# A one-element Gelu behind the last Exp, and one transposition placed a projection later

## The chip, the cores and the metric

The kernel runs on one core of a Trainium2 chip. The metric is the device time of one launch in microseconds (us). Three launches of the kernel before took 168.78, 169.01 and 170.12 us, so their median is 169.01 us. Trace times below count from the start of the profiled span.

## The reference

Attention over four batches with eight heads, 768 positions and a head size of 64, followed by a gated MLP block on its output. Attention keeps, for each query, the last 128 positions and the first four (sinks).

```python
scores = scale * np.matmul(q, k.transpose(0, 1, 3, 2))
scores = np.where(is_sink | in_window, scores, -1e9)
a = softmax(scores)
x = (a @ v)                     # as (4, 768, 512)
h = gelu_tanh(x @ w_in)         # w_in: 512 x 1024
u, v = h[..., :512], h[..., 512:]
v_n = (v - mean(v)) / sqrt(var(v) + 1e-6) * g_ln
v_s = einsum('ts,bsd->btd', w_sg, v_n) + b_sg
out = x + (u * v_s) @ w_out
```

## The kernel before

The 32 heads are worked off as 16 pairs (`n` = 0 to 15), four pairs to a batch, so "the fifteenth pair" is `n` = 14 and the last is 15. For each pair the kernel turns k and q so that the head size lies on the partitions, multiplies them into scores for three groups of keys (`score`), takes the exponential on ScalarE (L277, group 2 last), masks the band on VectorE and GpSimd (`keep_band`), and multiplies by v (`values(n, c)`, c = 0 and 1 for the two halves of the queries). `values` ends on VectorE: a reciprocal (L328) and a product that writes `x` (L329). Before the MLP can use `x` it has to be transposed into `xT`: by a DMA for pairs 8, 9, 12 and 13, and otherwise by `turn_x`, which is six transposing matmuls on TensorE into one bank (`xps`, L337) and one copy on VectorE or ScalarE (L341 or L339).

When a batch's four pairs are there, `hidden(b)` runs. `hidden_v` makes six tiles of the second half of h: four matmuls each over the chunks c = 0 to 3 of `xT` (three of them at L361, the last at L368), a Gelu on ScalarE into `v_all` (L370), and two statistics on VectorE (L372 `st`, L373 `mv`). Of these tiles the first three are opened ahead of time by `open_v`, which does L361 without L368. Then `hidden_u` makes eight half-width tiles of the first half (L380) with a Gelu each (L383, `uT`). `inverse_root` and `normalise` (L393 to L408, `vn`) are VectorE's. `spatial` multiplies `vn` by the turned `w_sg` (L418, six matmuls a tile, the sixth of which needs the sixth `vn`) and gates on VectorE (L421 `gv`, L424 `gT`). `project` multiplies by `w_out` (L449, four matmuls) and adds `x`, either on VectorE (L452) or by a fifth matmul (L455) with a copy on ScalarE (L458), and sends the tile out.

For batches 0 to 2, `spatial` and `project` are not run at once: they are put in a list, `fillers`, and `fill(k)` runs the next k of them between the steps of the next batch's attention. In the last batch the list holds, when the loop over pairs ends, projections of the batch before; those that add on VectorE come first and the three that copy on ScalarE last. The last call `fill(3)` inside `hidden(B - 1)` runs these three.

The schedule is manual: every engine runs its instructions in the order in which this code issues them. All TensorE results except scores go through four PSUM banks (`bank`, pool `ps_m`), given out in turn: a new tile waits until the tile four before it has been read. `hidden_v`, `turn_x`, `values`, `spatial` and `project` all take theirs from there.

ScalarE's functions need a table. In the loop it holds the one for Exp; the Gelus need another, loaded by an instruction of ScalarE (`ACT_TABLE_LOAD`) that the compiler places, so it carries the line of the instruction that it stands ahead of: L370, L277 or L223.

Around the change the order before, issued in the iteration n = 15 and behind the loop, is: a projection (called A here), `turn_x(14)`, then `fill()` (projection B), `values(15, 0)`, `values(15, 1)`, a third projection (C), `open_v` for tiles 0 and 1, `turn_x(15)`, `open_v` for tile 2, and `hidden`. A, B and C all add on VectorE.

Of the kernel before, what the change touches and what calls it, by code (L numbers as in the profile page):

```python
# [8 lines left out]
F32 = mybir.dt.float32  # L9
BF16 = mybir.dt.bfloat16  # L10
I32 = mybir.dt.int32
AF = mybir.ActivationFunctionType
# [6 lines left out]
def kernel(  # L19
# [15 lines left out]
    V, G, A = nc.vector, nc.gpsimd, nc.scalar  # L35
# [11 lines left out]
    NP = B * HP  # L47
# [9 lines left out]
    small = ctx.enter_context(tc.tile_pool(name="small", bufs=4))  # L57
# [15 lines left out]
    ones = consts.tile([128, 1], BF16, name="ones")  # L73
# [36 lines left out]
    def load_all(n):  # L110

        for which, m in (("k", n), ("q", n), ("v", n - 1)):
            if m < NP:
                load(m, which, in_rows=m >= FIRST)

    def cast_all(n, parts="kqv"):
        for which in parts:
            m = n - 1 if which == "v" else n
            if m < NP:
                cast(m, which, G)  # L120
# [27 lines left out]
    for i in range(WARM):  # L148
# [3 lines left out]
        out=halves[:, :, 0, :], in_=halves[:, :, 0, :], compare_op=ALU.is_ge, fill=DARK,  # L152
        base=0, pattern=[[0, 2], [1, 128]], channel_multiplier=-1)
    G.affine_select(
        out=halves[:, :, 1, :], in_=halves[:, :, 1, :], compare_op=ALU.is_ge, fill=DARK,
# [42 lines left out]
    def turn_weights(si, eng):  # L198
        ps = bank([128, NT, 128], BF16, "wps")
        for ti in range(NT):  # L200
            nc.tensor.transpose(ps[:, ti, :], wsg_sb[ti // HT][:, ti % HT, 128 * si:128 * (si + 1)],
                                iden)
        if eng is A:
            A.copy(wsgT[:, si, :], ps.rearrange("p t c -> p (t c)"))
        else:
            eng.tensor_copy(wsgT[:, si, :], ps.rearrange("p t c -> p (t c)"))


    def bank(shape, dtype, name):
        return ps_m.tile(shape, dtype, name=name, tag="m")  # L210
# [4 lines left out]
    def columns(n, which, eng):  # L215
        src = flat.pop((n, which))
        ps = bank([128, NT, 128], BF16, which + "ps")
        for t in range(NT):
            nc.tensor.transpose(ps[:, t, :], src[:, t, :], iden)  # L219
        dst = work.tile([128, S], BF16, name=which + "T")  # L220
        o, i = dst.rearrange("c (p t) -> c p t", t=NT), ps.rearrange("c t p -> c p t")
        if eng is A:
            A.copy(o, i)  # L223
        else:
            eng.tensor_copy(o, i)  # L225
        (kTs if which == "k" else qTs)[n] = dst
# [72 lines left out]
    def begin_x(b):  # L299
        x_sb[b] = work.tile([128, HP, NT, 128], BF16, name="x", bufs=3)  # L300
        xT[b] = work.tile([128, HP, S], BF16, name="xT")

    def values(n, c):
        b, hp = divmod(n, HP)
        if hp == 0 and c == 0:
            begin_x(b)
        ex, v_sb = exps[n], v_bufs[n % NV]
        av = bank([128, HT, 2, 65], F32, "av")

        def probs(j, l, half):  # L310
            at = 512 * l + 256 * (j % 2) + 128 * half
            return ex[:, j // 2, at:at + 128]

        first = True
        for m in range(HT):
            i = HT * c + m
            for l in range(2):
                for j, half in ((i, 0), (i - 1, 1)):
                    if j >= 0:
                        nc.tensor.matmul(av[:, m, l, :], probs(j, l, half), v_sb[:, l, j, :],  # L320
                                         start=first, stop=False)
                        first = False
        for l in range(2):
            sinks = ex[:, HT - 1, 512 * l + 384:512 * (l + 1)]
            to, of = (av[:, 2, l, :], 0) if c == 0 else (av[:, :, l, :], slice(1, 4))
            nc.tensor.matmul(to, sinks, vsink[:, of, n, l, :], start=False, stop=l == 1)  # L326
        rcp = rcps[:, n, c].rearrange("p (i l o) -> p i l o", l=2, o=1)
        V.reciprocal(rcp, av[:, :, :, 64:65])  # L328
        V.tensor_mul(  # L329
            x_sb[b][:, hp, HT * c:HT * (c + 1), :].rearrange("p i (l d) -> p i l d", l=2),  # L330
            av[:, :, :, 0:64], rcp.to_broadcast([128, HT, 2, 64]))

    def turn_x(n, eng):
        b, hp = divmod(n, HP)
        ps = bank([128, NT, 128], BF16, "xps")
        for t in range(NT):
            nc.tensor.transpose(ps[:, t, :], x_sb[b][:, hp, t, :], iden)  # L337
        if eng is A:
            A.copy(xT[b][:, hp, :], ps.rearrange("p t c -> p (t c)"))  # L339
        else:  # L340
            eng.tensor_copy(xT[b][:, hp, :], ps.rearrange("p t c -> p (t c)"))  # L341
# [33 lines left out]
    def hidden_u(b, f, n):  # L375
# [3 lines left out]
        for c in range(KD):  # L379
# [3 lines left out]
        A.activation(out=uTs[b][:, f, NH * n:NH * (n + 1)],  # L383
                     in_=h_ps[:, 0:NH], func=AF.Gelu_apprx_tanh)

    def inverse_root(b):

        w = small.tile([128, NT], F32, name="w", bufs=2)
        h = small.tile([128, NT], F32, name="h", bufs=2)
        s = small.tile([128, NT], F32, name="s", bufs=2)  # L390
        si = small.tile([128, NT], I32, name="si", bufs=2)
        y = small.tile([128, NT], F32, name="y", bufs=2)
        V.tensor_scalar(out=w, in0=mvs[b][:, :, 1], scalar1=1e-6, scalar2=None, op0=ALU.add)  # L393
        V.tensor_single_scalar(out=si, in_=w.bitcast(I32), scalar=1,
                               op=ALU.logical_shift_right)
        V.tensor_scalar(out=h, in0=w, scalar1=-0.5, scalar2=None, op0=ALU.mult)
        V.tensor_scalar(out=y.bitcast(I32), in0=si, scalar1=-1.0, scalar2=float(0x5f3759df),
                        op0=ALU.mult, op1=ALU.add)
        for _ in range(3):
            V.tensor_mul(s, y, y)  # L400
            V.tensor_mul(s, s, h)
            V.scalar_tensor_tensor(out=y, in0=s, scalar=1.5, in1=y, op0=ALU.add, op1=ALU.mult)
        rstds[b] = y
# [154 lines left out]
    def fill(count=1):  # L558
        for _ in range(count):
            if fillers:  # L560
                fillers.pop(0)()
# [117 lines left out]
    def x_by_dma(n):  # L679
        return n >= 2 * HP and n % HP < HP - 2  # L680
# [3 lines left out]
    for n in range(HP, NP):  # L684
        todo = valued < n - 1
        block = n % HP == 0 and n > HP
        if HP < n <= 2 * HP:
            load_all(n + 3)
        if n not in exps:
            score(n, 0, 1)  # L690
        if n == HP:
            for si in range(3, NT):
                turn_weights(si, V)
        keep_band(n, 0, V)
        keep_band(n, 1, G)
        if n + 2 >= FIRST:
            cast_all(n + 2, "kq")
        if todo:
            values(n - 1, 0)
        fill(2 if n > HP and not todo else 1)  # L700
        if n + 1 < FIRST and not block:
            columns(n + 1, "k", A)
        if n == HP:
            columns(n + 1, "q", V)
            fill()
        score(n, 2)
        keep_band(n, 2, G)
        if todo:
            values(n - 1, 1)
            if x_by_dma(n - 1):  # L710
                turn_x_by_dma(n - 1)
        if FIRST <= n + 2 < NP:
            columns_by_dma(n + 2)
            if n + 4 == FIRST + 2:
                load_all(n + 4)
        if QUOTA[n] > 2 and todo:
            fill()
        if HP < n < FIRST - 1 and not block:
            columns(n + 1, "q", A if todo else V)
        if n + 2 <= NP:  # L720
            cast_all(n + 2, "v" if n + 2 >= FIRST else "kqv")
        if QUOTA[n] > 1:
            fill()
        if block:
            open_v(n // HP - 1, 0)
            open_v(n // HP - 1, 1)
        if todo and not x_by_dma(n - 1):
            turn_x(n - 1, V)
        if block:
            open_v(n // HP - 1, 2)  # L730
        valued = n - 1
        if block:
            hidden(n // HP - 1, {1: [lambda: values(n, 0)], 3: [lambda: values(n, 1)],
                                 5: [lambda: columns(n + 1, "k", A)] if n + 1 < FIRST else [],
                                 6: [lambda m=m: load_all(m) for m in later.get(n, ())],
                                 7: [lambda: columns(n + 1, "q", A)] if n + 1 < FIRST else [],
                                 9: [lambda: turn_x_by_dma(n) if x_by_dma(n) else turn_x(n, V)],
                                 LAST: [lambda: score(n + 1, 0, 1), lambda: fill(2)]})
            valued = n
    fill()  # L740
    values(NP - 1, 0)
    values(NP - 1, 1)
    fill(len(fillers) - 3)
# [49 lines left out]
```

## Time and profile before

| what | us |
|---|---|
| median of three runs | 169.01 |
| profiled execution, whole | 168.79 |
| its span, first to last instruction | 167.0 |
| TensorE matmul busy | 155.6 (93%) |
| VectorE busy | 131.8 (79%) |
| ScalarE busy | 109.1 (65%) |
| GpSimd busy | 78.1 (47%) |
| table loads on ScalarE | 8, each 1.283 |
| span from 127.19 (last Exp ends) to 134.84 | ScalarE idle, 7.66 |

The span is 1.8 us shorter than the execution's time. The granted TensorE clock has a mean of 0.993 of full speed and is 1.00 in every stretch from 127 to 162 us. A matmul's end in the trace is modelled, and matmuls overlap: a start 0.216 us after the start before it is full pace for 512 columns and 0.162 us for 384, while the printed durations are 0.38 and 0.33. An idle time in brackets stands ahead of the instruction, with the one that ended it.

### The profile page before, as it was taken

The page shows a single profiled execution, that of the slowest core. Times are in us where ns is not written, and L with a number is a line of the kernel's source. Part 1 is how long each engine was busy: PE and PEld are TensorE (multiplying, and loading weights), DVE is VectorE, ACT ScalarE, POOL GpSimd, SP SyncE. Part 2 cuts the span into 40 slices and gives each one's busy share as a digit, 9 for nine tenths or more (in the row PEclk, how much of TensorE's full clock was granted, in tenths as well). Part 3 has the DMA queues.
Part 4 walks back from the last instruction along what each step waited for, and adds up shares of the span by engine and source line. Part 5 has one row for each costly group of instructions (what it writes and reads, how often), then busy time and mean ns, then how long its engine had stood idle before and what let it go on. Part 6 is the DMA issues. An engine that isn't in the chain of part 4 may idle for free.

```text
span 167.0 us, 4051 instructions
## 1 busy us (share of the span) xinstructions
PE 155.6 (93%) x1558; PEld 91.1 (55%) x1558; DVE 131.8 (79%) x317; ACT 109.1 (65%) x148; POOL 78.1 (47%) x115
## 2 busy tenths in 40 slices
PE   3979999999999999999999999999999989999960
PEld 3535574666567665565665655554565635545530
DVE  6756874996899986799888994989999939887620
ACT  3198878889977689688887367679754068621130
POOL 6479771105899979400289996001985000000000
PEclk9999999999999999999999999999999999999997
DMA  4999979999999979999903999899931310050343
GB/s 140 329 323 263 205 104 282 213 317 287 283 220 296 279 247 351 295 215 224 205 20 67 132 238 210 190 228 216 177 76 34 130 63 0 0 194 2 122 151 122
DMA packets 60194, 31.09 MB, mean 186 GB/s; under 512 B 48356, under 2 KB 57080, under 8 KB 60168
## 3 DMA queue, kind: packets, MB, share of 16 engines
q1 hardware_dynamic: 56800, 27.47, 68.8%
q0 software_dynamic: 2944, 2.77, 10.3%
q10 hardware_dynamic: 424, 0.53, 0.9%
q8 instruction: 14, 0.23, 0.6%
q14 instruction: 12, 0.10, 0.2%
HBM read 24.81 MB, written 6.29 MB: 186 GB/s over the span
## 4 chain that ended last, share of the span: by engine, by line
PE 70%; DVE 17%; DMA 5%; issue 1%; ACT 1%; SPq 1%; POOL 1%; POOLq 0%; ACTq 0%
PE vs L418 13%; PE o_ps L449 10%; PE hu L380 9%; PE hv L361 8%; PE av L320 7%; PE sc L264 6%; DMA k_sb<-in_k_dram 5%; DVE gT L424 3%; DVE gv L421 3%; PE hv L368 3%; PE xps L337 2%; DVE st L372 2%; PE av L326 2%; PE qps L219 2%; PE kps L219 2%; DVE vn L408 2%
## 5 line engine op out<-in xcount | busy, mean ns | idle before, releaser
L277 ACT ACTIVATE ex<-sc 128x1024 bf16<-128x1024 f32 x48 | 47.5, 1024 | 12.7 <-PE sc L264 9.2
L418 PE MATMUL vs<-wsgT,vn 128*128 128x384 bf16 x192 | 35.5, 326 | 0.1
L294 POOL TENSOR_SCALAR_AFFINE_SELECT ex<-ex 128x512 bf16<-128x512 bf16 x25 | 17.0, 680 | 30.7 <-issue 15.2
L418 PEld LDWEIGHTS <-vn 128*128 128x128 bf16 x192 | 17.7, 98 | 10.7 <-DVE tot L480 0.4
L449 PE MATMUL o_ps<-w_out_sb,gT 128*128 128x512 bf16 x92 | 23.5, 379 | 0.0
L380 PE MATMUL hu<-xT,w_in_sb 128*128 128x384 bf16 x128 | 22.1, 326 | 0.0
L421 DVE SCALAR_TENSOR_TENSOR gv<-vs,g_sb,b_bc 128x384 bf16<-128x384 f32 x32 | 19.6, 612 | 3.1 <-PE vs L418 2.7
L372 DVE BATCH_NORM_STATS2 st<-v_all 128x6 f32<-128x512 f32 x24 | 16.1, 671 | 5.8 <-ACT v_all L370 5.8
L361 PE MATMUL hv<-w_in_sb,xT 128*128 128x512 bf16 x72 | 18.8, 379 | 0.7 <-ACT v_all L370 0.7
L107 POOL CAST k_bf<-k_sb 128x768 bf16<-128x768 f32 x15 | 13.1, 870 | 13.0 <-DMA k_sb<-in_k_dram 9.0
L329 DVE TENSOR_TENSOR x<-av,rcps 128x384 bf16<-128x384 f32 x32 | 17.8, 557 | 1.1
L424 DVE TENSOR_TENSOR gT<-gv,uT 128x384 bf16<-128x384 bf16 x32 | 17.0, 532 | 1.9
L383 ACT ACTIVATE uT<-hu 128x384 bf16<-128x384 f32 x32 | 15.7, 493 | 4.1 <-PE hu L380 3.7
L458 ACT COPY o_sb<-o_ps 128x512 f32<-128x512 f32 x13 | 7.4, 593 | 14.3 <-PE o_ps L455 12.8
L264 PE MATMUL sc<-qT,kT 64*128 64x256 bf16 x192 | 15.7, 264 | 1.1 <-DVE qT L225 0.7
L380 PEld LDWEIGHTS <-w_in_sb 128*128 128x128 bf16 x128 | 12.3, 98 | 8.0
L370 ACT ACTIVATE v_all<-hv 128x512 f32<-128x512 f32 x24 | 13.1, 600 | 5.0 <-PE hv L368 4.6
L320 PE MATMUL av<-v_sb,ex 128*128 128x65 bf16 x352 | 16.1, 194 | 0.0
L104 POOL CAST v_sb<-v_sb 128x768 bf16<-128x768 f32 x16 | 14.5, 909 | 2.4 <-DMA v_sb<-in_v_dram 2.4
L320 PEld LDWEIGHTS <-ex 128*128 128x128 bf16 x352 | 13.1, 98 | 4.3 <-issue 1.1
L107 POOL CAST q_bf<-q_sb 128x768 bf16<-128x768 f32 x15 | 13.9, 925 | 2.9 <-DMA q_sb<-in_q_dram 2.9
L296 POOL TENSOR_SCALAR_AFFINE_SELECT ex<-ex 128x512 bf16<-128x512 bf16 (+1 forms) x25 | 14.4, 574 | 0.0
(88 smaller groups left out, 218.0 us busy)
## 6 DMA issues: line engine op xcount, KB each, us to landing
k_sb<-in_k_dram SPq DMA_DIRECT2D x16, 384.0 KB, 6.0
v_sb<-in_v_dram SPq DMA_DIRECT2D x16, 384.0 KB, 6.3
out_dram<-o_sb SPq DMA_DIRECT2D x23, 256.0 KB, 2.3
q_sb<-in_q_dram SPq DMA_DIRECT2D x15, 384.0 KB, 5.7
wsg_sb<-in_moe_w_sg_dram POOLq DMA_DIRECT2D x2, 576.0 KB, 10.9
w_in_sb<-in_moe_w_in_dram POOLq DMA_DIRECT2D x2, 256.0 KB, 6.4
w_in_sb<-in_moe_w_in_dram POOLq DMA_DIRECT2D x1, 512.0 KB, 5.4
w_out_sb<-in_moe_w_out_dram POOLq DMA_DIRECT2D x1, 512.0 KB, 9.3
```

The lines of the kernel that those rows point to most:

```text
L107: eng.tensor_copy(dst.rearrange("p t (h d) -> p h t d", h=2), src)
L264: nc.tensor.matmul(sc[:, 512 * l + w:512 * l + w + n_q], kT[rows, 128 * j:128 * (j + 1)], qT[rows, 128 * j:128 * j + n_q], start=not dark, ...
L277: A.activation(out=exps[n][:, g, :], in_=sc, func=AF.Exp, scale=scale)
L320: nc.tensor.matmul(av[:, m, l, :], probs(j, l, half), v_sb[:, l, j, :], start=first, stop=False)
L329: V.tensor_mul(x_sb[b][:, hp, HT * c:HT * (c + 1), :].rearrange("p i (l d) -> p i l d", l=2), av[:, :, :, 0:64], rcp.to_broadcast([128, HT ...
L361: nc.tensor.matmul(hvs[b, j], xT[b][:, c, 128 * j:128 * (j + 1)], w_in_sb[:, c, DF:], start=(c == 0), stop=False)
L372: V.bn_stats(out=st, in_=v_alls[b][:, j, :])
L380: nc.tensor.matmul(h_ps[:, 0:NH], w_in_sb[:, c, 128 * f:128 * (f + 1)], xT[b][:, c, NH * n:NH * (n + 1)], start=(c == 0), stop=(c == KD - 1))
L418: nc.tensor.matmul(vs[:, 0:NH], vns[b][:, si, 128 * f:128 * (f + 1)], wsgT[:, si, cols], start=(si == 0), stop=(si == NT - 1))
L421: V.scalar_tensor_tensor(out=gv, in0=vs[:, 0:NH], scalar=g_sb[:, f:f + 1], in1=b_bc[:, cols], op0=ALU.mult, op1=ALU.add)
L424: V.tensor_mul(gTs[b][:, f, cols], gv, uTs[b][:, f, cols])
L449: nc.tensor.matmul(o_ps, gTs[b][:, c, rows], w_out_sb[:, c, :], start=(c == 0), stop=(c == KU - 1 and not by_act))
```

## The change

```diff
+    def draw_gelu():
+
+        few = small.tile([1, 1], F32, name="few", bufs=1)
+        A.activation(out=few, in_=ones[0:1, :], func=AF.Gelu_apprx_tanh)
...
-        if todo and not x_by_dma(n - 1):
+        if todo and not x_by_dma(n - 1) and n < NP - 1:
             turn_x(n - 1, V)
...
             valued = n
+    draw_gelu()
     fill()
+    turn_x(NP - 2, V)
     values(NP - 1, 0)
     values(NP - 1, 1)
     fill(len(fillers) - 3)
```

Behind the loop over pairs, ScalarE gets one Gelu of a single element, whose result nothing reads. `turn_x(14)`, last in the iteration n = 15, is issued one projection later: the order becomes A, B, `turn_x(14)`, `values(15, 0)`, `values(15, 1)`, C. The Gelu's input `ones` was written at the start of the kernel.

In the instruction order of the two builds, ScalarE's stream gets one instruction more and the same number of table loads: the load that stood ahead of the first `v_all` of the last batch stands ahead of the one-element Gelu. Before, the load itself waited for TensorE and VectorE; it now waits for nothing, and the first `v_all` carries the waits. TensorE's six transpositions stand behind projection B's four matmuls, and VectorE's copy `xT` stands behind projection B's add. Nothing else changes place on any engine or queue. The branch that is taken only for inputs out of bounds keeps its work.

## The prediction

> **What bounds the kernel now.** I read the chain of waits first, for the stretch behind the last Exp. Its columns are start, length and what ran.
>
> ```profile
> 134.40 0.39 PE hv L368
> 134.79 0.03 ACTq L370
> 134.81 0.03 issue
> 134.84 1.28 ACT L370
> 136.12 0.01 issue
> 136.14 0.61 ACT v_all L370
> 136.74 0.02 issue
> 136.77 0.70 DVE st L372
> ...
> 145.24 2.83 DVE vn L408 x6
> 148.07 0.07 DVE tot L480
> 148.14 4.23 PE vs L418 x25
> ```
>
> The table load of 1.28 us lies on the chain: it starts when the first hv is written and the Gelu starts 0.02 behind it. From 136.77 to 148.07 VectorE runs without a gap to the sixth vn; there TensorE takes the chain over and, by the later rows, holds it to 161.47, when one copy and a DMA are left. Next is the timeline, to see how far TensorE trails VectorE at that handover, and how an earlier batch did it.
>
> ```profile
> 103.18 2.31 ACT L370 ACTIVATE v_all<-hv 128x512 f32<-128x512 f32 x4 [0.79 <-PE hv L368]
> 134.84 1.28 ACT L370 ACT_TABLE_LOAD   x1 [7.66 <-PE hv L368]
> 135.69 0.38 PE L368 MATMUL hv<-w_in_sb,xT 128*128 128x512 bf16 x1
> 136.78 0.81 PE L361 MATMUL hv<-w_in_sb,xT 128*128 128x512 bf16 x3 [0.72 <-ACT v_all L370]
> 146.73 0.38 PE L455 MATMUL o_ps<-x,iden 128*128 128x512 bf16 x1
> 147.14 5.23 PE L418 MATMUL vs<-wsgT,vn 128*128 128x384 bf16 x30
> ```
>
> In the third batch the load ran at 101.11, before hv was due, and the first Gelu began 0.42 behind the start of hv's last matmul (102.76 to 103.18). In the last batch that distance is 1.76 (134.38 to 136.14). TensorE suffers too: its fifth hv tile waits for the bank that the first Gelu reads.
>
> Last, the timeline around the moved transposition.
>
> ```profile
> 128.41 0.56 DVE L329 TENSOR_TENSOR x<-av,rcps 128x384 bf16<-128x384 f32 x1
> 129.02 0.34 PE L337 MATMUL xps<-iden,x 128*128 128x128 bf16 x3 [0.28 <-DVE x L329]
> 129.80 0.68 DVE L452 TENSOR_TENSOR o_sb<-o_ps,x 128x512 f32<-128x512 f32 x1
> 130.40 0.55 DVE L341 COPY xT<-xps 128x768 bf16<-128x768 bf16 x1
> 130.54 0.53 PE L320 MATMUL av<-v_sb,ex 128*128 128x65 bf16 x12
> 130.87 0.68 DVE L452 TENSOR_TENSOR o_sb<-o_ps,x 128x512 f32<-128x512 f32 x1
> 131.07 1.02 PE L449 MATMUL o_ps<-w_out_sb,gT 128*128 128x512 bf16 x4
> ```
>
> TensorE waits 0.28 for x, but VectorE has no gap here: it goes from one row into the next. That decides the second part.
>
> **The change part by part.** *The Gelu.* Load and Gelu go where ScalarE sits idle for 7.66 us (127.19 to 134.84). The load is 1.28. A one-element Gelu is not in the trace: nothing from below, since it is an added instruction, and 0.37 from above (the smallest ScalarE row, the copy of 256 columns at L441); I take 0.2, from the 493 ns of 384 columns and 1024 ns of 1024, which extrapolate to 0.17 at none. Together 1.5 of 7.66, so 6.2 us of cover remain and the cost is nothing. Were that cover gone, it would be 1.5 on ScalarE's path. No ScalarE work is queued behind them before the first v_all, which now waits itself; the row for such a wait is the 0.03 + 0.03 between hv and the load, paid already. Its bounds are 0.06 saved and 0.06 added; I take zero. So the first v_all comes at 136.14 - 1.30 = 134.84 if hv is no later.
>
> The Trainium skill, ScalarE: Activation LUTs, section What ACT_TABLE_LOAD costs, puts a switch at 1283 ns for the load and about 1380 ns more for a drain, some 2.66 us. The load's 1.283 agrees; the 0.02 between its end and the Gelu, and the 0.03 of issue ahead of it, leave no room for the drain here. By the page the sum would gain an estimated 1.38 us more.
>
> *The transposition.* A's four matmuls start at 127.55, so B's start at 127.55 + 4 x 0.216 = 128.41. B takes a bank that a gv read free at 127.61 (127.00 + 0.61). B ends its share at 129.28, x was written at 128.97, so the 0.28 wait is gone and the six transpositions end by about 129.65. But the second values(15) tile takes A's bank, which A's add frees at 129.80 + 0.68 = 130.48. It started at 130.54 before and cannot start sooner now: the 0.28 turns into a wait for that add. Then projection C, which took the bank of xps (free at 130.95), takes B's, freed by B's add. On VectorE the add and the copy trade places: add 130.40 to 131.08, copy about 131.00 to 131.55; the reciprocal behind them stays at 131.47. So C starts at about 131.08 + 0.05 = 131.13 where it started at 131.07: 0.06 lost. The first open_v takes the bank of xps, free at 131.55, and starts at 131.94 + 0.06 = 132.00, with 0.45 to spare; its third matmul, the first to read the moved xT, has more. x of the last pair is written at 132.94 as before, ahead of its transposition at 133.29. The move is therefore worth -0.06, with bounds of +0.20 (if TensorE were free of VectorE, x at 132.94 would let the last transposition start near 133.0, not 133.23) and -0.45.
>
> *What it sums to.* hv is 0.06 later, so the first v_all is at 134.90, 1.24 earlier. VectorE has v_all tiles in time (six in 3.17, while its own statistics take 0.81 a tile and a 1.1 us count lies between), so the sixth vn ends at 148.07 - 1.24 = 146.83. TensorE: the fourth hv's last matmul starts at 135.69, so without the bank wait the fifth tile starts at 135.69 + 0.216 = 135.90, plus 0.06 = 135.96; the bank is free at about 134.90 + 0.61 + 0.02. The gain is 136.78 - 135.96 = 0.82, for the hu tiles and the three projections alike, as no row between shows TensorE waiting for the statistics. TensorE's first vs matmul moves from 147.14 to 146.32 and the sixth would be 5 x 0.162 behind it, at 147.13. vn is there at 146.83. So TensorE, not VectorE, now sets the end, and its sixth vs matmul moves from 148.14 to 147.13: 1.01 us. Everything behind is TensorE's chain, with VectorE following it at 0.98 a tile, so the shift goes through to the last DMA. What is late next is TensorE itself, by 0.3 us.
>
> 168.79 - 1.01 = 167.78 us, against the profiled execution. That execution is 0.22 below the median of the runs, so a median is likelier between 167.8 and 168.0.
>
> **The rivals.** *Nothing lands, 168.85.* The compiler puts the load where a table is needed; a second load ahead of v_all, or a wait left on the load, would leave 134.84 to 136.12 as it is and add the 0.06 of the move. For it: in the batch before the change the load carried the wait itself. Against: the eight loads of the profile stand one to a change of function; six v_all, eight uT and the copies between run on one, as at 101.11, and in the built order the only load left stands ahead of the small Gelu. The Trainium skill, ScalarE activation tables: per-element evaluation and per-set limits, section Table sets in the compiler and the runtime, has the loads placed per block by the longest run, which fits these rows.
>
> *More, 167.55 or less.* VectorE's 1.24 comes through whole if TensorE makes up 0.23 between 136 and 147. For it: the count's matmul (L478) starts 0.31 behind L455 rather than 0.216, and some such pauses may close. Against: TensorE's rows from 138.51 to 147 follow each other at full pace. The drain of the page, as a mechanism here, would be 1.38 between load and Gelu; the 0.02 speaks against it, and I give it 1 in 100 within this case.
>
> *Slower, 169.4.* One mechanism: projection B, now ahead of the transpositions, finds its bank not yet free. If it got A's turn of banks and waited for A's add (130.48), B would start at 130.53. From B's start to the first open_v it is 0.86 + 0.34 + 1.01 + 0.86 = 3.07 at the pace of the rows (projection, transpositions, values from 130.06 to 131.07, projection): 133.60 in place of 131.94. That is 1.66 lost; ScalarE's part alone still gives 0.88 + 0.19 = 1.07 (TensorE's bank wait, and the 148.14 - 147.95 that it now waits for vn), so 0.59 slower. It costs something once B starts later than about 131.94 + 0.06 - 3.07 = 128.93, and makes the kernel slower once later than 131.94 + 1.07 - 3.07 = 129.94. Against: banks go round by four and B's was freed at 127.61. For: these rounds are tight, as A's bank shows.
>
> **How the numbers follow.** The forecast gets 0.65; nothing lands 0.12; more 0.13; slower 0.10. The forecast's own range is 167.5 to 168.1 by the bounds above, of which the move's ends are the widest, with 0.2 for the median. The range of 167.3 to 169.0 adds the no-gain case and most of "more", and leaves out the slower one. One per cent of the median, about what a measurement of this kernel can tell from no change, is 1.69 us: below 167.32 lies part of "more" and a low draw of the forecast, 0.10; above 170.70 lies the tail of "slower", 0.06; the rest, 0.84, is within.
>
> **What would show it.** In the profile after: the load behind the last Exp at about 127.2; no load ahead of the last batch's v_all, and that v_all near 134.9; no wait of the fifth hv tile for ScalarE; the sixth vn near 146.8 and TensorE not waiting for it; C at 131.1 and open_v at 132.0. Wrong would be a first vs matmul still at 147.1, which says that TensorE kept its place, or VectorE still ahead of the sixth vs in the chain, which is "more".

## The result and the profile after

The changed kernel takes 167.95 us (median of 14 runs, 167.29 to 169.05) against 168.88 us for the kernel before, measured beside it. The ratio is 0.994, with a 95% interval of 0.992 to 0.996: 0.9 us faster, with 167.8 forecast for the profiled execution. Some executions of the versions below were slower as a whole, by 1.5% or more, and the ratios leave them out. The profiled execution takes 167.96 us, 0.83 less than the one before; its span is 166.15 us in the trace, where it was 166.95 (the table of the profile before rounds it to 167.0). Lines behind the new function are five to seven higher: L418 is now L423, L449 is L454.

The chain of waits, for the stretch shown before (start, length, what ran):

```profile
133.63 0.65 PE hv L361 x3
134.28 0.01 issue
134.28 0.82 PE hv L368 x3
...
137.69 5.20 PE hu L380 x32
...
146.22 4.98 PE vs L423 x30
```

ScalarE and VectorE are gone from this stretch. TensorE runs from hv through hu, the three projections and all thirty vs matmuls without a break. The timeline shows where the load went:

```profile
127.03 1.28 ACT L389 ACT_TABLE_LOAD   x1
...
128.33 0.20 ACT L389 ACTIVATE few<-ones 1x1 f32<-1x1 bf16 x1
...
134.76 2.71 ACT L370 ACTIVATE v_all<-hv 128x512 f32<-128x512 f32 x5 [6.23 <-issue]
...
135.80 0.81 PE L361 MATMUL hv<-w_in_sb,xT 128*128 128x512 bf16 x3
...
143.87 2.83 DVE L413 TENSOR_SCALAR vn<-v_all,mv,y 128x512 bf16<-128x512 f32 x6
...
146.16 5.05 PE L423 MATMUL vs<-wsgT,vn 128*128 128x384 bf16 x30
```

The fifth hv tile (135.80) has no wait for ScalarE any more. The six vn end at 143.87 + 2.83 = 146.70, and TensorE takes the sixth 0.81 behind 146.16. And the moved transposition:

```profile
127.37 1.89 PE L454 MATMUL o_ps<-w_out_sb,gT 128*128 128x512 bf16 x8
...
129.10 0.50 PE L337 MATMUL xps<-iden,x 128*128 128x128 bf16 x6
...
129.64 1.28 DVE L457 TENSOR_TENSOR o_sb<-o_ps,x 128x512 f32<-128x512 f32 x2
...
130.38 0.53 PE L320 MATMUL av<-v_sb,ex 128*128 128x65 bf16 x12 [0.41 <-DVE o_sb L457]
...
130.84 0.55 DVE L341 COPY xT<-xps 128x768 bf16<-128x768 bf16 x1
...
130.97 1.02 PE L454 MATMUL o_ps<-w_out_sb,gT 128*128 128x512 bf16 x4
```

A and B run as one row of eight, the wait for x is gone, and in its place TensorE waits 0.41 for A's add. This add is the one VectorE step left on the chain behind the last Exp.

Executions differ in what happens before this stretch. Projection A's first matmul stands between 127.36 and 127.82 in eleven of the thirteen profiled executions of this study, and at 128.75 and 128.79 in the other two (e4 and e5 below). In those two the granted TensorE clock was 0.50 from 14 to 16 us, where the other eleven have 1.00; their executions took 169.80 and 169.49 us, about 1 us more than the medians of the same versions. What moves the other eleven by up to 0.5 us was not followed up. So the traces are compared from A's first matmul on:

| from A's first matmul | before | forecast change | measured change |
|---|---|---|---|
| to projection C | 3.52 | +0.06 | 3.60, +0.08 |
| to the first v_all | 8.59 | -1.24 | 7.39, -1.20 |
| to the fifth hv tile | 9.23 | -0.82 | 8.43, -0.80 |
| to the first vs matmul | 19.59 | -0.82 | 18.79, -0.80 |
| to the last copy on ScalarE ("the stretch") | 33.94 | -1.01 | 32.96, -0.98 |
| from that copy to the end of the span | 5.46 | 0 | 5.82, +0.36 |

With A itself 0.18 earlier, 0.18 + 0.98 - 0.36 = 0.80 us is the difference of the two spans. Of these three only the 0.98 is in the forecast's sum. The 0.18 is chance: the changed kernel, run again (after_again below), has A at 127.59.

### The profile page after: what moved, and what is told of

It reads as the page before. It is cut to its first block, busy times and chain, and to the rows that moved or that the text cites. A ratio compares the mean times of both kernels' runs of the same rounds, so it can differ in the third digit from the quotient of the medians.

```text
span 166.1 us, 4052 instructions
## 1 busy us (share of the span) xinstructions
PE 155.0 (93%) x1558; PEld 91.2 (55%) x1558; DVE 132.6 (80%) x317; ACT 109.4 (66%) x149; POOL 78.0 (47%) x115
## 4 chain that ended last, share of the span: by engine, by line
PE 80%; DMA 6%; POOL 3%; DVE 3%; SPq 3%; issue 1%; ACT 0%; POOLq 0%
PE vs L423 15%; PE hu L380 13%; PE o_ps L454 12%; PE hv L361 9%; PE av L320 7%; PE sc L264 7%; DMA q_sb<-in_q_dram 4%; PE hv L368 4%; SPq L95 3%; PE xps L337 2%; DMA qT<-q_bf 2%; PE av L326 2%; PE qps L219 2%; PE kps L219 2%; PE o_ps L460 2%; PE sc L247 2%
## 5 line engine op out<-in xcount | busy, mean ns | idle before, releaser
L423 PE MATMUL vs<-wsgT,vn 128*128 128x384 bf16 x192 | 35.3, 326 | 0.1
L423 PEld LDWEIGHTS <-vn 128*128 128x128 bf16 x192 | 17.8, 98 | 10.4
L454 PE MATMUL o_ps<-w_out_sb,gT 128*128 128x512 bf16 x92 | 23.2, 379 | 0.0
L107 POOL CAST k_bf<-k_sb 128x768 bf16<-128x768 f32 x15 | 12.6, 837 | 12.8 <-DMA k_sb<-in_k_dram 12.7
L286 DVE TENSOR_TENSOR ex<-ex,mask 128x1024 bf16<-128x1024 bf16 x14 | 13.1, 939 | 2.3 <-ACT ex L277 2.1
```

What stands on the lines that cost most here:

```text
L107: eng.tensor_copy(dst.rearrange("p t (h d) -> p h t d", h=2), src)
L423: nc.tensor.matmul(vs[:, 0:NH], vns[b][:, si, 128 * f:128 * (f + 1)], wsgT[:, si, cols], start=(si == 0), stop=(si == NT - 1))
L454: nc.tensor.matmul(o_ps, gTs[b][:, c, rows], w_out_sb[:, c, :], start=(c == 0), stop=(c == KU - 1 and not by_act))
```

## The experiments

The theory is the forecast's: the Gelu brings 0.88 from TensorE's wait for the first hv's bank and 0.19 from its wait for the sixth vn, the move costs 0.06, and TensorE alone sets the end afterwards. Its rivals: the move has a share in the gain, and VectorE's chain is what counts. All diffs are against the changed kernel unless they say otherwise. "Stretch" is from A's first matmul to the start of the last ScalarE copy, in one profiled execution of each version; the changed kernel, profiled twice, has 32.96 and 32.95.

| run | stretch expected | stretch measured | ratio to before (95% interval) |
|---|---|---|---|
| e1_gelu_only | 32.87 | 32.91 | 0.996 (0.994 to 0.999) |
| e2_turn_only | 34.00 | 34.01 | 1.002 (1.000 to 1.005) |
| e3_after_count_early | 32.96 | 32.95 | 0.996 (0.994 to 0.998) |
| e4_before_count_early | 33.75 | 33.76 | 1.000 (0.997 to 1.003) |
| e5_first_by_act | 32.67 | 32.68 | 0.994 (0.990 to 0.998) |
| e6_rows_by_dve | 32.53 | 32.54 | 0.990 (0.985 to 0.995) |
| e7_all_rows | 31.81 | 31.86 | 0.991 (0.988 to 0.995) |
| e8_act_old_turn | 32.8 | 32.93 | 0.994 (0.991 to 0.998) |
| after_again | 32.96 | 32.95 | 0.994 (0.990 to 0.997) |
| e9_act_rows | 32.26 | 32.24 | 0.990 (0.986 to 0.995) |
| e10_row3_act_queue | 31.86 | 31.86 | 0.992 (0.989 to 0.996) |

**The two parts apart.** First the Gelu alone:

```diff
-        if todo and not x_by_dma(n - 1) and n < NP - 1:
+        if todo and not x_by_dma(n - 1):
             turn_x(n - 1, V)
...
     fill()
-    turn_x(NP - 2, V)
```

> The one-element Gelu alone, turn_x(14) in its old place. Measure in the trace: from projection A's first matmul to the start of the last copy on ScalarE, 33.94 us before the change and 32.96 us after it. Theory (the Gelu brings everything, the move costs 0.06): 1.07 us shorter than before the change, about 32.87, and 0.1 us faster than the changed kernel; TensorE waits 0.28 for x of pair 14 again and does not wait for A's add. Rival (the move brings a part, or the Gelu needs it): 33.2 or more, 0.3 us or more slower than the changed kernel.

Then the move alone, shown against the kernel before:

```diff
-        if todo and not x_by_dma(n - 1):
+        if todo and not x_by_dma(n - 1) and n < NP - 1:
             turn_x(n - 1, V)
...
     fill()
+    turn_x(NP - 2, V)
     values(NP - 1, 0)
```

> The moved turn_x(14) alone, without the Gelu. Theory: 0.06 us longer than before the change, 34.00 in the stretch from A to the last copy, a ratio of 1.000; the load stands at about 134.9 in the chain again and the wait of 0.28 for x has become a wait of about 0.4 for A's add. Rival (the 0.28 is saved): 33.66, 0.28 us faster.

The Gelu alone has its wait for x back and its last copy at 160.47, which is 32.91 behind A at 127.56. In its timeline:

```profile
129.06 0.34 PE L337 MATMUL xps<-iden,x 128*128 128x128 bf16 x3 [0.31 <-DVE x L329]
...
131.11 1.02 PE L454 MATMUL o_ps<-w_out_sb,gT 128*128 128x512 bf16 x4
...
160.47 0.37 ACT L446 COPY o_last<-o_ps 128x256 f32<-128x256 f32 x1 [0.35 <-PE o_ps L445]
```

The move alone, with A at 127.68, shows the wait for A's add and the load in its old place:

```profile
130.68 0.53 PE L320 MATMUL av<-v_sb,ex 128*128 128x65 bf16 x12 [0.41 <-DVE o_sb L452]
...
131.28 1.02 PE L449 MATMUL o_ps<-w_out_sb,gT 128*128 128x512 bf16 x4
...
135.05 1.28 ACT L370 ACT_TABLE_LOAD   x1 [7.73 <-PE hv L368]
...
136.99 0.81 PE L361 MATMUL hv<-w_in_sb,xT 128*128 128x512 bf16 x3 [0.72 <-ACT v_all L370]
```

The Gelu is worth 33.94 - 32.91 = 1.03 us and the move 34.01 - 33.94 = +0.07 by itself, +0.05 behind the Gelu. C stands 3.55 behind A in the first run and 3.60 in the second. The timed medians of these two versions, 167.85 and 169.07 us, lie on the same sides of the 168.90 for the kernel before. Differences of 0.05 to 0.2 us are inside the intervals, so only the traces show them, here and for the early count below.

**Which engine carries the gain.** The count (four VectorE steps of 1.1 us between the third and the fourth statistics) is issued ahead of `hidden`, into VectorE's gap:

```diff
-    hidden(B - 1, {2: [lambda: seen.update(c=count_good())],
-                   LAST: [lambda: fill(3)]})
+    seen["c"] = count_good()
+    hidden(B - 1, {LAST: [lambda: fill(3)]})
```

> The changed kernel with the four VectorE steps of the count issued ahead of hidden, into VectorE's gap of 1.16 us before the first statistics, so that the sixth vn comes about 1.1 us earlier. Theory (TensorE alone sets the end after the change, with the sixth vn 0.3 us early): no change, 32.96 in the stretch, within 0.1 us. Rival (VectorE's chain still sets the end): up to 1.1 us faster, 31.9.

The same edit was made to the kernel before:

> The kernel before the change with the count issued early in the same way. The load stays on the chain, but the sixth vn comes 1.1 us earlier. Theory (of the change's gain 0.19 is TensorE's wait for the sixth vn and 0.88 its wait for the bank of the first hv): 0.19 us faster than before, 33.75 in the stretch, and the wait of 0.72 for the Gelu stays. Rival (the chain through VectorE is what the load delays): 1.0 us or more faster, 32.9, without any table work.

In the changed kernel with the early count, vn and vs are:

```profile
143.16 2.83 DVE L413 TENSOR_SCALAR vn<-v_all,mv,y 128x512 bf16<-128x512 f32 x6
...
146.59 5.05 PE L423 MATMUL vs<-wsgT,vn 128*128 128x384 bf16 x30
```

A started at 127.82 here, so the sixth vn comes 18.17 behind it instead of 19.33: 1.16 earlier. vs starts at 18.77 instead of 18.79. So VectorE was ahead by a whole microsecond more and nothing followed. In the kernel before with the early count (A at 128.75) it is:

```profile
137.99 0.81 PE L361 MATMUL hv<-w_in_sb,xT 128*128 128x512 bf16 x3 [0.72 <-ACT v_all L370]
...
145.31 2.83 DVE L408 TENSOR_SCALAR vn<-v_all,mv,y 128x512 bf16<-128x512 f32 x6
...
148.34 5.05 PE L418 MATMUL vs<-wsgT,vn 128*128 128x384 bf16 x30
```

The vs matmuls take 5.05 as they do after the change, not 5.23: the wait for the sixth vn is gone, which is worth 33.94 - 33.76 = 0.18. The bank wait of 0.72 stays, and with it the other 0.85 of the Gelu's 1.03: with the Gelu alone, the first vs matmul starts 18.74 behind A, 0.85 sooner than the 19.59 before. That splits the gain as the sum had it, with 0.85 and 0.18 for 0.88 and 0.19.

**The new wait.** Projection A gets ScalarE's form, a fifth matmul and a copy, so that its bank is read out sooner:

```diff
-            fillers.extend(lambda t=t: project(b, t, t % 2 == 1) for t in (0, 2, 4, 1, 3, 5))
+            fillers.extend(lambda t=t: project(b, t, t % 2 == 1 or (b == B - 2 and t == 0))
+                           for t in (0, 2, 4, 1, 3, 5))
```

> The changed kernel, in which projection A adds x by a fifth matmul and is copied by ScalarE (idle there), so that its bank is free about 1 us earlier and VectorE has 0.6 us less ahead of values(15). It costs TensorE 0.216. Theory (the wait of 0.41 before the second values(15) tile is for A's bank, and behind it the two VectorE steps in a row): the wait goes, C starts about 0.29 earlier, 32.67 in the stretch from A to the last copy (32.96 without). Rival (that wait is for something else on VectorE): longer by 0.2, 33.17.

The wait goes and the stretch is 32.68, by 0.28 shorter although TensorE has one matmul more. In its timeline (A at 128.79) the load now follows the copy, still far ahead of the first v_all:

```profile
130.07 0.58 ACT L463 COPY o_sb<-o_ps 128x512 f32<-128x512 f32 x1 [1.64 <-PE o_ps L460]
...
130.68 1.28 ACT L389 ACT_TABLE_LOAD   x1
...
131.44 0.53 PE L320 MATMUL av<-v_sb,ex 128*128 128x65 bf16 x12
...
131.98 1.03 PE L454 MATMUL o_ps<-w_out_sb,gT 128*128 128x512 bf16 x4
...
151.41 0.36 DVE L429 TENSOR_TENSOR gT<-gv,uT 128x384 bf16<-128x384 bf16 x1 [0.46 <-DVE gv L426]
```

C is 3.19 behind A, not 3.60, so 0.41 was gained there; vs starts at 18.37, 0.42 earlier. The rest was lost in the gating stage, where the third gT starts 0.46 late (last line) and the next projection's four matmuls take 1.16 instead of 1.03. This also stands in the traces of e7, e8, e9 and e10, all with this edit, and in none without it. Why is open. So the expected 32.67 was met partly by luck: C came 0.41 earlier, 0.12 more than the expected 0.29, and the late gT, which was not expected, took back about 0.14.

With the same edit and `turn_x(14)` in its old place:

> The Gelu, projection A on ScalarE, and turn_x(14) in its old place. Theory (once A's bank is free early, the old place still waits for x until 129.02, so the moved turn is worth what it was meant for): 32.8, that is 0.1 shorter than the Gelu alone (32.91) and 0.13 longer than the same with the turn moved. Rival (the place of the turn does not matter, or costs 0.06 as before): 32.67 or less.

It is 32.93, that is 0.25 longer than with the turn moved. The same late gT is in it, which that expectation did not have in its sum: 32.8 + 0.13 is what was measured. So the move is worth 0.25 once A's bank is free early, and costs 0.05 to 0.07 as long as it is not.

**Less work for TensorE.** In the last batch the second and third whole projections get their add on VectorE:

```diff
-        rows = [lambda t=t: project(b, t, t != HT) for t in range(NT - 1)]
+        rows = [lambda t=t: project(b, t, t in (0, 4)) for t in range(NT - 1)]
```

> The changed kernel, in which the second and third projections of the last batch add x on VectorE instead of by a fifth matmul and a copy on ScalarE: 2 x 0.216 less on TensorE, 2 x 0.6 more on VectorE, into gaps of 0.95 and 0.92 us. Theory (TensorE alone sets the end from 146 on): 0.43 shorter, 32.53. Rival (VectorE, which follows it closely, takes over): 32.96 or longer.

Two matmuls less, 0.42 shorter. With the edit of A, and all whole projections of the last batch so (`project(b, t, False)`):

> Projection A on ScalarE as in the first run of this set, and all five whole projections of the last batch with their add on VectorE, four of them new there: 4 x 0.216 less on TensorE. Theory: 0.29 + 0.86 shorter, 31.81, if VectorE's gaps (0.39, 0.95, 0.92 us and the one before the last add) hold the four adds. Rival (VectorE becomes the bound in this stage): about 32.3 or longer, with TensorE waiting for gT or for a bank.

The stretch is 1.10 shorter than the changed kernel's, but the span only 0.40 (165.75): from the last copy to the end it takes 165.75 - 159.22 = 6.53 us, not 5.82. In SyncE's queue the issue of the fifth output (the time the queue spends on giving out the transfer) is long, and the first half of the last tile stands behind it, though its add ends at 158.90 + 0.41 = 159.31:

```profile
159.01 1.51 SPq L464 DMA_DIRECT2D out_dram<-o_sb  x1
...
160.61 0.38 SPq L447 DMA_DIRECT2D out_dram<-o_last  x1
```

The long issue does not explain the late end by itself, though. e6 has one nearly as long, and its end is not late (165.71 - 159.98 = 5.73 us):

```profile
159.66 1.36 SPq L464 DMA_DIRECT2D out_dram<-o_sb  x1
```

To compare on one chip, the changed kernel was run again beside the last two versions:

> The changed kernel once more, so that the versions beside it are compared on the same chip. Both theories: 32.96 us in the stretch from projection A to the last copy on ScalarE, and a ratio to the kernel before of about 0.994.

Both savings, with only the second and third projections on VectorE:

> The changed kernel with projection A on ScalarE and the adds of the second and third projections of the last batch on VectorE. Theory (the two savings are on TensorE's chain one behind the other and add up: 0.28 and 0.42): 32.26 in the stretch. Rival for the whole time (behind the last copy the output DMAs set the end, so what TensorE saves is lost there): the stretch is 32.26, but from the last copy's start to the end it takes 6 us or more where the changed kernel takes 5.8, and the median is that of the changed kernel.

And the version with all adds on VectorE, one output on ScalarE's queue:

```diff
-        nc.sync.dma_start(out=out[b, rows, :], in_=o_sb)
+        (A if b == B - 1 and t == HT else nc.sync).dma_start(out=out[b, rows, :], in_=o_sb)
```

> Projection A on ScalarE and all five whole projections of the last batch with their add on VectorE (31.86 in the stretch as measured), with the fourth one's output DMA issued by ScalarE's queue. With all on SyncE, the fifth output's issue took 1.51 us where 0.33 is usual, and the last half waited behind it until 160.61, 1.3 us after its data was there. Theory (the long issue comes of three outputs on one queue within 1.5 us): SyncE's issue is back at about 0.4, the last half is issued within 0.2 us of its add, and the kernel is up to 1 us faster than the changed one, a ratio of 0.988. Rival (it is the transfers' engines, whatever the queue): the issue stays over 1 us, and the ratio is 0.991.

The fifth output is issued in 0.33 again, and the issue of the first half starts 0.12 behind its add, as the theory had it. But then the last two halves, one on each queue, take long, and the kernel gains nothing by it:

```profile
159.32 0.33 SPq L464 DMA_DIRECT2D out_dram<-o_sb  x1
...
159.74 1.34 SPq L447 DMA_DIRECT2D out_dram<-o_last  x1
...
159.93 1.14 ACTq L447 DMA_DIRECT2D out_dram<-o_last  x1
```

From the last copy to the end it is 166.29 - 159.52 = 6.77. So long issues come on either queue. Nor is it enough that outputs come close together: in the versions that leave this stage alone the fifth output is always issued 0.96 behind the fourth, and takes anything from 0.33 (the changed kernel) to 1.21 (e8). What holds an issue, and what makes the end late in e7 and e10, stays open. In e9 one takes 1.46:

```profile
159.46 1.46 SPq L464 DMA_DIRECT2D out_dram<-o_sb  x1
```

Yet its end takes 5.83, so its rival did not come true in the trace (span 165.62). Over the executions that the ratios use, its median is 167.67 beside 168.21 for the changed kernel on the same chip, with ratios to the kernel before of 0.990 (0.986 to 0.995) and 0.994 (0.990 to 0.997): e6 and e9 are faster than the kernel before, clear of the noise, and have shorter stretches than the changed kernel, but in time their lead over it is not clear of the noise.

## Why the prediction was right

*The load is on the chain and the last Exp leaves room for it.* Right: 1.28 + 0.20 us in an idle time of 7.66. The small Gelu's 0.2, taken from the rows of larger ones, was measured as 0.20. The first v_all waits for TensorE itself and follows hv's last matmul by 0.48 (134.28 to 134.76), where 0.46 stood ahead of the load before; the extra waits that it carries cost 0.02 at most.

*No second load, and no drain.* The Trainium skill, ScalarE activation tables: per-element evaluation and per-set limits, section Table sets in the compiler and the runtime, places loads by the longest run in a block; the trace agrees, with one load in the last batch for the small Gelu, six v_all and eight uT. The Trainium skill, ScalarE: Activation LUTs, section What ACT_TABLE_LOAD costs, adds about 1.38 us of drain to a switch. Here the next instruction starts 128.33 - 127.03 - 1.28 = 0.02 behind the load, and the gain was 1.03, not 2.4: the drain is not in these traces.

*The gain is TensorE's, not VectorE's.* Right, and the step that mattered most, since the first v_all came 1.20 us earlier and the end only 0.98. The early count in both kernels shows it from two sides.

*The move turns a wait for x into a wait for A's bank.* Right: 0.28 became 0.41, at a cost of 0.05 to 0.07 where the sum had 0.06.

*What lies behind the last copy moves along unchanged.* This was the loosest step. The same code took 5.5 to 6.3 us there over the profiled executions that leave this stage alone, with the output DMAs' issues taking 0.33 to 1.2 us, so a part of a small gain can disappear in it: 0.36 did in the profiled execution, and the 0.18 by which A happened to come earlier hid half of that. The two medians differ by 0.93, so on the whole little was lost.

*The range.* The bounds of the forecast's own range do not follow from its terms: a move worth +0.20 or -0.45 instead of -0.06 gives 167.52 and 168.17, and 168.37 with the 0.2 for the median, not 168.1. The measured 167.95 lies inside all of these.

None of the rivals came true. "Nothing lands" falls with the load at 127.03, "more" with TensorE's unbroken chain, and "slower" with B's start directly behind A.

## What to carry to other kernels

When an engine's setup step sits between a producer and its consumer, look at whether it began when the engine became idle or when the data came; a step that needs no data can be drawn ahead by a dummy user of it, and what that is worth is read at the next place where two engines meet, not from the step's length. Before moving work to fill a wait, follow the buffers given out behind it: here the transposition's own wait went, and the next tile waited for a bank that an add still held, so the move paid only together with an earlier read-out of that bank. When an engine has become the only bound, taking instructions from it pays at full price as far as it stays the bound, here up to the last copy; behind that, with the output transfers, a part of the gain was lost again in two of four versions.

## What the runs showed of the hardware

The issue of the last batch's 256 KB outputs took 0.33 or 0.34 us on SyncE in most cases. The fifth of them took 0.33 to 1.21 us in nine profiled executions in which it stood 0.96 us behind the fourth each time, and 1.36, 1.46 and 1.51 us in e6, e9 and e7; in e10 two 128 KB halves took 1.34 us on SyncE and 1.14 us on ScalarE's queue. What holds an issue stays open. In all five versions with the edit of e5 a VectorE product started 0.46 us late with no other engine named as the reason; it was not followed up.

In two of thirteen profiled executions the granted TensorE clock was 0.50 from 14 to 16 us, and projection A, far behind it, came about 1 us later than in the others.
